# Fewer first-layer matmuls through take-outs, in a spectral-mixing and squared-ReLU kernel: 96 slots in fixed patterns, with new orders on three engines

## The chip, the cores and the metric

The kernel runs on one core of one Trainium2 chip. The metric is the device time of one execution in microseconds (us), lower is better. Each comparison runs the kernel before and the changed ones in turn on the same chip; different comparisons ran on different chips. The names of the engines in the profile are: PE for TensorE's matmuls and PEld for its weight loads, DVE for VectorE, ACT for ScalarE, POOL for GpSimd, SP for the engine that issues most DMAs. An "L" with a number is a line of the kernel.

## The reference

A real part of a two-dimensional Fourier transform over sequence and features, then a feed-forward layer with a squared ReLU.

```python
# x: (8, 3008, 256) f32; w_in: (256, 2048); w_out: (2048, 256)
X = np.fft.fft(np.fft.fft(x, axis=1), axis=2).real
x2 = X.reshape(8 * 3008, 256)
h = np.maximum(x2 @ w_in, 0.0)
out = (h * h) @ w_out           # (24064, 256) f32
```

## The kernel before

The feature transform is folded into the first weights (`G1`, `G2`, `G3`), the sequence transform makes two tables per batch, `pt` and `qt`. Column i of them serves two tokens, i and its mirror image: with A = G1 x pt and B = G2 x qt one token needs A+B, the other A-B. The 12040 columns are cut into 25 chunks. Chunks 2 to 23 have 512 columns and 8 slots each; a slot makes 256 of the 2048 hidden features for a chunk. The second layer's matmuls (`po`) of one chunk are spread over the slots of the next.

An ordinary slot uses three matmuls per 128 features: `G1` and `G2` give A+B, ScalarE reads it from PSUM, where the matmuls' results lie; `G3` (twice `G2`, negative, with other signs in one edge row) turns it into A-B, ScalarE reads again. A *take-out* slot saves the third one: after `G1`, VectorE takes A out of PSUM, doubled and with a correction for the edge row (`t`), TensorE adds `G2`, ScalarE reads A+B, and VectorE reads A+B again with `t` to make A-B. The correction is an *edge term* (`et`), made by POOL: a row of `qt`, spread to all 128 partitions by a DMA once per chunk (`eb`), times a number per feature.

```python
    def e_spread(c):                       # POOL issues the copy of the chunk's edge row
        ebc[c] = esp.tile([P, CH], F16, name="eb", tag="eb", bufs=2)
        for (b, i, o, l) in chunks[c][3]:
            nc.gpsimd.dma_start(out=ebc[c][:, o : o + l],
                in_=PQ[b][1][P - 1 : P, i : i + l].unsqueeze(1).to_broadcast([1, P, l]))
    def e_term(c, u):                      # two POOL multiplies of 128x512
        t = edge[c, u] = esp.tile([P, 2, CH], F16, name="et", tag="et", bufs=2)
        for j in range(2):
            f = 2 * u + j
            nc.gpsimd.tensor_scalar(out=t[:, j], in0=ebc[c], scalar1=gE2[:, f : f + 1],
                                    scalar2=None, op0=ALU.mult)
    # ... (x_front: G1, then VectorE takes out)
            stt(out=t, in0=xb, scalar=-2.0, in1=edge.pop((c, u)), op0=ALU.mult, op1=ALU.add)
    # ... (x_back, a take-out: TensorE has added G2)
        nc.vector._custom_dve(TENSOR_ADD_SAT, out=d[:, :, ::-1], in0=v, in1=t, s0=BIG, s1=0.0)
        act(r_s(c, u), v, AF.Relu, scale=-1.0)
    # ... (when they are issued; si is the step of slot u of chunk c)
    for si, (c, u) in enumerate(steps):
        if u == 0 and PLAN[c][0]:
            side.setdefault(si - (2 if len(chunks[c][3]) > 1 else 4), []).append(lambda c=c: e_spread(c))
    for si, (c, u) in enumerate(steps):
        if u in PLAN[c][0]:
            side.setdefault(si - 2, []).append(lambda c=c, u=u: e_term(c, u))
```

The schedule is manual: every engine runs its instructions in the order of this code. So a wait of POOL for one thing holds up everything behind it on POOL.

Of the kernel before, what the change touches and what calls it, by code (L numbers as in the profile page):

```python
# [10 lines left out]
F32 = mybir.dt.float32  # L11
F16 = mybir.dt.float16
I32 = mybir.dt.int32
AF = mybir.ActivationFunctionType
# [10 lines left out]
def kernel(  # L25
# [7 lines left out]
    nc = tc.nc  # L33
    B, S, D = x.shape
    _, F = moe_w_in.shape
    P = 128
# [10 lines left out]
    NFC = F // P  # L47
# [27 lines left out]
    def iota(name, shape, pattern, base, mult, dt=F32):  # L75
        t = const.tile(shape, dt, name=name)
        nc.gpsimd.iota(t, pattern=pattern, base=base, channel_multiplier=mult,
                       allow_small_or_imprecise_dtypes=True)
        return t
# [49 lines left out]
    for s in range(2):  # L129
        gather(0, 1 - s)  # L130
        nc.sync.dma_start(out=x4[0:NP, s, :, :], in_=up(0, s))
    jrow = iota("jrow", [P, P], [[1, P]], 1, 0)
    idx2 = iota("idx2", [P, 1], [[0, 1]], NQ // 2 * (NP - 1), -NQ // 2, I32)
    wout16 = const.tile([P, NFC, D], F16, name="wout16")
    wst = [h2p.tile([P, 2, F // 4], F32, name="wst", tag="h2") for _ in range(4)]
# [53 lines left out]

    def dmats():  # L190
        pv = nc.gpsimd
        t = tgp.tile([P, P], F32, name="td", tag="td")
        m = tgp.tile([P, P], F32, name="md", tag="md")
        pv.tensor_scalar(out=m, in0=jrow, scalar1=pidx[:, 0:1], scalar2=None, op0=ALU.mult)
        pv.tensor_scalar(out=t, in0=m, scalar1=1.0 / D, scalar2=R23, op0=ALU.mult, op1=ALU.add)
        pv.tensor_scalar(out=t, in0=t, scalar1=R23, scalar2=-float(D),
                         op0=ALU.subtract, op1=ALU.mult)
        pv.tensor_tensor(m, m, t, op=ALU.add)
        pv.memset(csD[:, 0, 0, P - 1 : P], 1.0)

        def fin():
            absval(t, m)
            nc.vector.tensor_copy(csD[:, 0, 1, P - 1 : P], alt)
            act(csD[:, 0, 1, 0 : P - 1], m[:, 0 : P - 1], AF.Sin, bias=0.0, scale=wD)
            act(csD[:, 0, 0, 0 : P - 1], t[:, 0 : P - 1], AF.Sin, bias=hpi[:, 0:1], scale=-wD)

        def hi():
            ts(out=csD[:, 1, :, 0:P:2], in0=csD[:, 0, :, 0:P:2], scalar1=-1.0, scalar2=None,
               op0=ALU.mult)
            nc.vector.tensor_copy(csD[:, 1, :, 1:P:2], csD[:, 0, :, 1:P:2])  # L210
        return fin, hi
# [270 lines left out]
        chunks.append((g, n, CH // n, segs, NFC // (2 * (CH // n))))  # L482
        g += n

    YZ = [(0, 0)] * 4 + [(3, 0)] * 2 + [(4, 1)] * 9 + [(5, 2)] * 9 + [(0, 0)]

    def plan(c, y, z):
        n = chunks[c][4]
        if chunks[c][1] != CH:
            return (), ()  # L490
        return ([u for u in range(n) if (u * y + 4) % n < y],
                [u for u in range(n) if (u * z + 6) % n < z])

    PLAN = [plan(c, *YZ[c]) for c in range(len(chunks))]

# [12 lines left out]
    def h2v(c, u):  # L508
        n, nf = chunks[c][1:3]
        if (c, u) not in h2t:  # L510
            t = h2p.tile([P, 4 * CH], F16, name="h2", tag="h2")
            h2t[c, u] = t[:, 0 : 4 * nf * n].rearrange("p (f t) -> p f t", f=2 * nf)
        return h2t[c, u]

    def mm2_ops(c):
        g0, n, nf, segs, _ = chunks[c]
        full = n // P * P
        tiles = [(s, t0, P) for s in range(2) for t0 in range(0, full, P)]
        groups = [tiles[i : i + 2] for i in range(0, len(tiles), 2)]
        if n > full:  # L520
            groups.insert(0, [(2, full, n - full)])
        ops = []
        st = {}

        def rows_out(s, t0, m, src):
            base = g0 + n - t0 - m if s else g0 + t0
            o = 0
            while o < m:
                b, i = divmod(base + o, NK)
                if i < NE:  # L530
                    l = min(m - o, NE - i)
                    kk = 2 * i
                else:
                    l = min(m - o, NK - i)
                    kk = 2 * (i - NE) + 1
                lo, hi = 0, l
                if s and kk == 0:
                    lo = 1
                if s and kk + 2 * (l - 1) == M:
                    hi = l - 1  # L540
                if hi > lo:
                    if s:
                        r0 = b * S + S - (kk + 2 * (hi - 1))
                        p0 = m - (o + hi)
                    else:
                        r0 = b * S + kk + 2 * lo
                        p0 = o + lo
                    nl = hi - lo
                    nc.sync.dma_start(out=out[r0 : r0 + 2 * nl - 1 : 2, :], in_=src(p0, nl))
                o += l  # L550

        def store(grp, po):
            os_ = osp.tile([P, 2, D], F32, name="os", tag="os")
            if grp[0][0] == 2:
                _, t0, m = grp[0]
                act(os_[0 : 2 * m, 0], po[0 : 2 * m, 0], AF.Copy, bias=0.0, scale=HS * HS)
                rows_out(0, t0, m, lambda p0, nl: os_[p0 : p0 + nl, 0, :])
                rows_out(1, t0, m, lambda p0, nl: os_[m + p0 : m + p0 + nl, 0, :])
                return
            act(os_, po, AF.Copy, bias=0.0, scale=HS * HS)  # L560
            for j, (s, t0, m) in enumerate(grp):
                rows_out(s, t0, m, lambda p0, nl, j=j: os_[p0 : p0 + nl, j, :])

        def one(grp, j, fc):
            s, t0, m = grp[j]

            def f():
                if j == 0 and fc == 0:
                    st["o"] = pso.tile([P, 2, D], F32, name="po", tag="po")
                o = n + n % P + t0 if s == 1 else t0  # L570
                w = 2 * m if s == 2 else m
                mm(st["o"][0:w, j, :], h2v(c, fc // (2 * nf))[:, fc % (2 * nf), o : o + w], wout16[:, fc, :],
                   fc == 0 and j == 0, fc == NFC - 1)
                if fc == NFC - 1 and j == len(grp) - 1:
                    return lambda o=st["o"]: store(grp, o)
            return f

        for grp in groups:
            ops += [one(grp, j, fc) for j in range(len(grp)) for fc in range(NFC)]
        return ops  # L580

    def relu_d(c, u, put):
# [9 lines left out]
    def r_s(c, u):  # L592
        return h2v(c, u)[:, :, 0 : chunks[c][1]]
# [24 lines left out]
    edge = {}  # L618

    def e_term(c, u):  # L620
        t = edge[c, u] = esp.tile([P, 2, CH], F16, name="et", tag="et", bufs=2)
        for j in range(2):
            f = 2 * u + j
            nc.gpsimd.tensor_scalar(out=t[:, j], in0=ebc[c], scalar1=gE2[:, f : f + 1], scalar2=None,  # L624
                                    op0=ALU.mult)
# [18 lines left out]
    def x_back(cur):  # L644
        c, u, xb, t = cur
        for j in range(2 * chunks[c][2]):
            x_mm(c, u, xb, j, G3 if t is None else G2, 1, False)
        v = x_view(c, xb)
        if t is None:
            relu_d(c, u, lambda o, i: act(o, v[:, :, i], AF.Relu, scale=-1.0))  # L650
            return
        d = h2v(c, u)[:, :, CH : 2 * CH]
        nc.vector._custom_dve(TENSOR_ADD_SAT, out=d[:, :, ::-1], in0=v, in1=t, s0=BIG, s1=0.0)  # L653
        act(r_s(c, u), v, AF.Relu, scale=-1.0)  # L654

    def x_square(cur):
        c, u = cur[:2]
# [108 lines left out]
    side.setdefault(10, []).append(e_double)  # L766
    for si, (c, u) in enumerate(steps):
        if u == 0 and PLAN[c][0]:
            side.setdefault(si - (2 if len(chunks[c][3]) > 1 else 4), []).append(lambda c=c: e_spread(c))
    for si, (c, u) in enumerate(steps):  # L770
        if u in PLAN[c][0]:
            side.setdefault(si - 2, []).append(lambda c=c, u=u: e_term(c, u))

    LAG = 1
    SQ = 1
# [7 lines left out]
    def retire():  # L783
        v = made.pop(0)
        x_square(v)
        if v[1] == chunks[v[0]][4] - 1:
            wait.append(v[0])

    for si, (c, u) in enumerate(steps):
        while wait:  # L790
            d = wait.pop(0)
            mmq += mm2_ops(d)
            due = si + chunks[d + 1][4]
        take = [mmq.pop(0) for _ in range(-(-len(mmq) // max(1, due - si)))]
        h = len(take) // 2
        posts = []
        if si in turn:
            posts += [f() for f in take[:h]]
        flight.append(x_front(c, u))
        if si not in turn:  # L800
            posts += [f() for f in take[:h]]
        if len(flight) > LAG:
            x_back(flight[0])
            made.append(flight.pop(0))
        posts += [f() for f in take[h:]]
        for p in posts:
            if p:
                p()
        while rest:
            rest.pop()()  # L810
        if len(made) > SQ:
            retire()
        for f in side.get(si, []):
            f()
    while flight:
# [42 lines left out]
```

## Time and profile before

| | before |
|---|---|
| median of the runs beside the changed kernel | 641.87 us (641.72 to 645.73, 4 runs) |
| span in the profile | 641.1 us |
| take-outs (edge terms) / ScalarE squares | 87 / 27 |

The page of the kernel before, part 1 (busy time of each engine, share of the span, instructions) and part 4 (the chain of waits that ended last, followed back from the end: share of the span by engine, then by engine and line):

```profile
PE 598.3 (93%) x4606; PEld 439.0 (68%) x4606; DVE 523.8 (82%) x650; ACT 417.9 (65%) x525; POOL 396.6 (62%) x269
...
PE 50%; DVE 12%; POOL 12%; DMA 7%; issue 5%; ACT 3%; DVEq 0%; SPq 0%; POOLq 0%; ACTq 0%
PE po L73 29%; PE xb L73 17%; POOL et L624 9%; DMA x<-in_x_dram 3%; DVE h L664 3%; DMA eb<-qt 3%; PE pf L73 3%; DVE h L653 2%; DVE t L639 2%; POOL x L101 2%; DVE u L328 2%; ACT h L650 1%; DVE v L340 1%; POOL x L124 1%; ACT os L560 1%
```

TensorE is the bound, but 12% of the chain lies on edge terms and the copies that feed them (9% + 3%).

The groups of instructions of the kernel before (count, then busy us, mean ns; then the idle time just before them and what ended it):

```profile
L73 PE MATMUL po<-wout,h 128*128 128x256 f16 x3024 | 394.1, 273 | 6.0 <-DVE h L664 6.0
L624 POOL TENSOR_SCALAR et<-eb,gE 128x512 f16<-128x512 f16 x174 | 327.9, 1897 | 106.3 <-DVE t L639 53.2
L653 DVE CUSTOM_DVE_ANT_0 h<-xb,t 128x1024 f16<-128x1024 f32 x87 | 106.2, 1221 | 29.4 <-PE xb L73 29.2
L639 DVE SCALAR_TENSOR_TENSOR t<-xb,et 128x1024 f32<-128x1024 f32 x87 | 105.9, 1219 | 18.8 <-POOL et L624 15.2
```

A take-out thus costs VectorE 1.22 + 1.22 us and POOL 2 x 1.90 us. The wait list of the kernel before (who waited for whom: us in total, times, longest):

```profile
ACT h L654 <- DVE h L653: 122.3, 77, 5.3
...
POOL et L624 <- DVE t L639: 53.2, 27, 3.8
POOL et L624 <- DMA eb<-qt: 46.5, 12, 7.8
...
DVE t L639 <- POOL et L624: 15.2, 12, 3.7
```

The timeline of POOL in the kernel before (start us, duration us, what, how many; in brackets the idle time before it and what ended it). The first copy here is for chunk 21, which straddles two batches and needs two; the others are for chunks 22 and 23:

```profile
525.37 3.10 POOL L624 TENSOR_SCALAR et<-eb,gE 128x512 f16<-128x512 f16 x2 [2.07 <-DVE t L639]
528.42 1.14 POOL L615 DMA_DIRECT2D eb<-qt  x2
535.72 14.13 POOL L624 TENSOR_SCALAR et<-eb,gE 128x512 f16<-128x512 f16 x8 [6.16 <-DMA eb<-qt]
549.80 0.59 POOL L615 DMA_DIRECT2D eb<-qt  x1
550.44 3.10 POOL L624 TENSOR_SCALAR et<-eb,gE 128x512 f16<-128x512 f16 x2
556.93 13.39 POOL L624 TENSOR_SCALAR et<-eb,gE 128x512 f16<-128x512 f16 x8 [3.40 <-DMA eb<-qt]
570.27 0.58 POOL L615 DMA_DIRECT2D eb<-qt  x1
571.77 3.10 POOL L624 TENSOR_SCALAR et<-eb,gE 128x512 f16<-128x512 f16 x2 [0.91 <-DVE t L639]
577.04 7.00 POOL L624 TENSOR_SCALAR et<-eb,gE 128x512 f16<-128x512 f16 x4 [2.18 <-DMA eb<-qt]
```

A copy's *flight*, from its issue to its landing, takes over 6 us (6.6 in the median, part 6 of the page). In chunk 21 nothing stands between issue and first term, and POOL idles 6.16 us. In chunks 22 and 23 one term of the chunk before (two multiplies, 3.1 us) stands between, and POOL idles 3.40 and 2.18 us.

### The profile page before, as it was taken

To read this page: it belongs to the slowest core of one execution; us is meant where nothing else is said; L and a number is where in the kernel's file an instruction comes from. 1 tells how busy PE (TensorE), PEld (TensorE's weight loads), DVE (VectorE), ACT (ScalarE), POOL (GpSimd) and SP (SyncE) were. 2 spreads that over 40 slices of the span, in tenths; PEclk is the share of its full clock that TensorE was granted. 3 is DMA by queue.
4 is the path that set the end of the run, shared out by engine and by line. 5 is a ranking of instruction groups with operands and counts; after the bars stand their busy time and mean duration, and the time that the engine had idled before them with its cause. 6 is when DMAs were issued, how large, how long until landed. Compare 5 with 4: busy or idle time off the path is not lost.

```text
span 641.1 us, 11481 instructions
## 1 busy us (share of the span) xinstructions
PE 598.3 (93%) x4606; PEld 439.0 (68%) x4606; DVE 523.8 (82%) x650; ACT 417.9 (65%) x525; POOL 396.6 (62%) x269
## 2 busy tenths in 40 slices
PE   3867998979999999899999999999999999999997
PEld 1545676656777777667777767866777767877786
DVE  8787696998898989789899879788787886888730
ACT  5865676455666676566765665766766676777771
POOL 8303043773778749978686758867587676789100
PEclk9989999899999999999999999999999999999999
DMA  8955367874196142941333131331431313431112
GB/s 264 295 93 135 110 159 198 147 186 83 51 179 116 50 58 38 221 69 51 46 55 41 52 40 52 59 42 34 58 48 45 58 50 42 58 57 52 50 51 67
DMA packets 37259, 57.05 MB, mean 89 GB/s; under 512 B 7214, under 2 KB 31442, under 8 KB 37206
## 3 DMA queue, kind: packets, MB, share of 16 engines
q0 software_dynamic: 7456, 30.08, 28.9%
q1 hardware_dynamic: 29702, 26.23, 13.0%
q8 instruction: 36, 0.59, 0.4%
q14 instruction: 17, 0.14, 0.1%
q10 hardware_dynamic: 48, 0.02, 0.0%
HBM read 29.02 MB, written 24.64 MB: 84 GB/s over the span
## 4 chain that ended last, share of the span: by engine, by line
PE 50%; DVE 12%; POOL 12%; DMA 7%; issue 5%; ACT 3%; DVEq 0%; SPq 0%; POOLq 0%; ACTq 0%
PE po L73 29%; PE xb L73 17%; POOL et L624 9%; DMA x<-in_x_dram 3%; DVE h L664 3%; DMA eb<-qt 3%; PE pf L73 3%; DVE h L653 2%; DVE t L639 2%; POOL x L101 2%; DVE u L328 2%; ACT h L650 1%; DVE v L340 1%; POOL x L124 1%; ACT os L560 1%
## 5 line engine op out<-in xcount | busy, mean ns | idle before, releaser
L73 PE MATMUL po<-wout,h 128*128 128x256 f16 x3024 | 394.1, 273 | 6.0 <-DVE h L664 6.0
L624 POOL TENSOR_SCALAR et<-eb,gE 128x512 f16<-128x512 f16 x174 | 327.9, 1897 | 106.3 <-DVE t L639 53.2
L73 PEld LDWEIGHTS <-h 128*128 128x128 f16 x3024 | 289.4, 98 | 98.2 <-DVE h L664 9.0
L664 DVE TENSOR_TENSOR h<-h 128x2048 f16<-128x2048 f16 (+1 forms) x165 | 201.2, 1220 | 16.2 <-ACT h L650 15.1
L73 PE MATMUL xb<-qt,G 128*128 128x512 f16 (+16 forms) x796 | 190.1, 321 | 9.3 <-DVE t L639 4.7
L654 ACT ACTIVATE h<-xb 128x1024 f16<-128x1024 f32 x87 | 89.2, 1025 | 123.9 <-DVE h L653 122.3
L73 PEld LDWEIGHTS <-G 128*128 128x128 f16 x1308 | 119.3, 98 | 69.8 <-issue 19.9
L73 PE MATMUL xb<-pt,G 128*128 128x512 f16 (+16 forms) x512 | 131.2, 323 | 10.0 <-ACT h L654 3.2
L653 DVE CUSTOM_DVE_ANT_0 h<-xb,t 128x1024 f16<-128x1024 f32 x87 | 106.2, 1221 | 29.4 <-PE xb L73 29.2
L641 ACT ACTIVATE h<-xb 128x1024 f16<-128x1024 f32 (+1 forms) x105 | 104.4, 994 | 33.4 <-PE xb L73 33.1
L650 ACT ACTIVATE h<-xb 128x1024 f16<-128x1024 f32 (+1 forms) x113 | 104.9, 937 | 29.5 <-PE xb L73 29.0
L639 DVE SCALAR_TENSOR_TENSOR t<-xb,et 128x1024 f32<-128x1024 f32 x87 | 105.9, 1219 | 18.8 <-POOL et L624 15.2
L560 ACT ACTIVATE os<-po 128x512 f32<-128x512 f32 x94 | 56.0, 596 | 9.4 <-PE po L73 6.3
L124 POOL DMA_DIRECT2D x<-in_x_dram x14 | 8.2, 586 | 78.8 <-DVE u L332 77.8
L328 DVE TENSOR_TENSOR u<-x 127x765 f16<-127x765 f32 x32 | 30.4, 975 | 5.5 <-DMA x<-in_x_dram 4.8
L101 POOL DMA_INDIRECT x<-in_x_dram,idx x18 | 27.8, 1545 | 5.5 <-issue 4.5
L662 ACT ACTIVATE h<-h 128x1024 f16<-128x1024 f16 x27 | 28.6, 1061 | 0.0
L661 ACT ACTIVATE h<-h 128x1024 f16<-128x1024 f16 x27 | 28.5, 1055 | 0.0
L73 PEld LDWEIGHTS <-w 127*128 127x128 f16 (+1 forms) x192 | 22.5, 120 | 8.6 <-DVE w L346 1.6
L346 DVE TENSOR_TENSOR w<-v 127x381 f16<-127x381 f16 x64 | 22.6, 385 | 0.0
L396 ACT ACTIVATE as<-pf 128x377 f32<-128x377 f32 (+5 forms) x32 | 15.6, 487 | 8.0 <-PE pf L73 6.6
L73 PE MATMUL pf<-cosT,w 127*128 127x377 f16 (+1 forms) x96 | 19.2, 336 | 0.8 <-DVE w L346 0.8
(101 smaller groups left out, 199.1 us busy)
## 6 DMA issues: line engine op xcount, KB each, us to landing
out_dram<-os SPq DMA_DIRECT2D x157, 128.0 KB
x<-in_x_dram POOLq DMA_DIRECT2D x14, 756.0 KB, 10.6
wst<-in_moe_w_in_dram POOLq DMA_DIRECT2D x4, 512.0 KB, 7.2
wot<-in_moe_w_out_dram POOLq DMA_DIRECT2D x4, 512.0 KB
eb<-qt POOLq DMA_DIRECT2D x14, 128.0 KB, 6.6
x<-in_x_dram SPq DMA_DIRECT2D x2, 756.0 KB
x<-in_x_dram,idx POOLq DMA_INDIRECT x18, 12.0
gE<-G SPq DMA_DIRECT2D x16, 0.2 KB
```

The source lines that it names most:

```text
L73: nc.tensor.matmul(o, l, r, start=start, stop=stop, skip_group_check=True)
L101: nc.gpsimd.indirect_dma_start(out=x4[0:NP, 2 + s, q : q + rows, :].rearrange("p q d -> p (q d)"), out_offset=None, in_=bass.AP(tensor=x.t ...
L328: return lambda: vt(u[k, s, q0 : q0 + NQ // 2, 1:D], x4[k, s, q0 : q0 + NQ // 2, 1:D], x4[k, 3 - s, ::-1, :][:, q0 : q0 + NQ // 2, D - 1 : ...
L560: act(os_, po, AF.Copy, bias=0.0, scale=HS * HS)
L624: nc.gpsimd.tensor_scalar(out=t[:, j], in0=ebc[c], scalar1=gE2[:, f : f + 1], scalar2=None, op0=ALU.mult)
L639: stt(out=t, in0=xb, scalar=-2.0, in1=edge.pop((c, u)), op0=ALU.mult, op1=ALU.add)
L641: act(r_s(c, u), x_view(c, xb), AF.Relu, scale=-1.0)
L650: relu_d(c, u, lambda o, i: act(o, v[:, :, i], AF.Relu, scale=-1.0))
L653: nc.vector._custom_dve(TENSOR_ADD_SAT, out=d[:, :, ::-1], in0=v, in1=t, s0=BIG, s1=0.0)
L654: act(r_s(c, u), v, AF.Relu, scale=-1.0)
L662: rest.append(lambda: act(h2[:, nf:], h2[:, nf:], AF.Square))
L664: vt(h2, h2, h2, op=ALU.mult)
```

## The change

Its intent: nine more take-outs, to spare TensorE matmuls; to pay for them on VectorE and POOL with better orders: ScalarE reads the sums first, squares move ahead of the VectorE sum, terms are made three steps ahead into three buffers, the second layer uses the last tile late.

```diff
-    YZ = [(0, 0)] * 4 + [(3, 0)] * 2 + [(4, 1)] * 9 + [(5, 2)] * 9 + [(0, 0)]
+    TAKE = {0: (), 3: (1, 4, 6), 4: (1, 3, 4, 6), 5: (1, 2, 4, 5, 6), 6: (0, 1, 2, 4, 5, 6)}
+    SQA = {0: (), 1: (4,), 2: (1, 5), 3: (1, 4, 6)}
+    YZ = [(0, 0)] * 4 + [(3, 0)] * 2 + [(5, 1)] * 18 + [(0, 0)]
 ...   (before, slots by formula: y=3: 2 4 7; y=4: 1 3 5 7; y=5: 0 1 3 4 6)
         for grp in groups:
-            ops += [one(grp, j, fc) for j in range(len(grp)) for fc in range(NFC)]
+            for fcs in (range(NFC - 2 * nf), range(NFC - 2 * nf, NFC)):
+                ops += [one(grp, j, fc) for j in range(len(grp)) for fc in fcs]
 ...
-        t = edge[c, u] = esp.tile([P, 2, CH], F16, name="et", tag="et", bufs=2)
+        t = edge[c, u] = esp.tile([P, 2, CH], F16, name="et", tag="et", bufs=3)
 ...
+        act(r_s(c, u), v, AF.Relu, scale=-1.0)
         nc.vector._custom_dve(TENSOR_ADD_SAT, out=d[:, :, ::-1], in0=v, in1=t, s0=BIG, s1=0.0)
-        act(r_s(c, u), v, AF.Relu, scale=-1.0)
 ...
-            side.setdefault(si - (2 if len(chunks[c][3]) > 1 else 4), []).append(lambda c=c: e_spread(c))
+            one = len(chunks[c][3]) == 1
+            late = chunks[c][3][-1][0] - 1 in EGRP
+            side.setdefault(si - (4 if one else 2 if late else 3), []).append(lambda c=c: e_spread(c))
 ...
-            side.setdefault(si - 2, []).append(lambda c=c, u=u: e_term(c, u))
+            side.setdefault(si - 2 - (u > 0), []).append(lambda c=c, u=u: e_term(c, u))
 ...
         if si in turn:
-            posts += [f() for f in take[:h]]
+            posts += [f() for f in take]
+            take = []
         flight.append(x_front(c, u))
-        if si not in turn:
-            posts += [f() for f in take[:h]]
+        posts += [f() for f in take[:h]]
+        if len(made) > SQ - 1:
+            retire()                 # the square, ahead of the VectorE sum (before: after it)
         if len(flight) > LAG:
             x_back(flight[0])
```

Cut: two small scratch tiles of the start move into a buffer that is free then, which makes room for the third `et` buffer.

More of the change, by code (lines that the diff above doesn't have):

```diff
@@ L131 @@
         nc.sync.dma_start(out=x4[0:NP, s, :, :], in_=up(0, s))
-    jrow = iota("jrow", [P, P], [[1, P]], 1, 0)
+    jm = h2p.tile([P, 3, P], F32, name="jm", tag="h2")
+    jrow = jm[:, 0]
+    nc.gpsimd.iota(jrow, pattern=[[1, P]], base=1, channel_multiplier=0,
+                   allow_small_or_imprecise_dtypes=True)
     idx2 = iota("idx2", [P, 1], [[0, 1]], NQ // 2 * (NP - 1), -NQ // 2, I32)
@@ L191, in dmats @@
         pv = nc.gpsimd
-        t = tgp.tile([P, P], F32, name="td", tag="td")
-        m = tgp.tile([P, P], F32, name="md", tag="md")
+        t, m = jm[:, 1], jm[:, 2]
         pv.tensor_scalar(out=m, in0=jrow, scalar1=pidx[:, 0:1], scalar2=None, op0=ALU.mult)
@@ L483 @@
         g += n
-    YZ = [(0, 0)] * 4 + [(3, 0)] * 2 + [(4, 1)] * 9 + [(5, 2)] * 9 + [(0, 0)]
+    TAKE = {0: (), 3: (1, 4, 6), 4: (1, 3, 4, 6), 5: (1, 2, 4, 5, 6), 6: (0, 1, 2, 4, 5, 6)}
+    SQA = {0: (), 1: (4,), 2: (1, 5), 3: (1, 4, 6)}
+    YZ = [(0, 0)] * 4 + [(3, 0)] * 2 + [(5, 1)] * 18 + [(0, 0)]
     def plan(c, y, z):
-        n = chunks[c][4]
-        if chunks[c][1] != CH:
-            return (), ()
-        return ([u for u in range(n) if (u * y + 4) % n < y],
-                [u for u in range(n) if (u * z + 6) % n < z])
+        return TAKE[y], SQA[z]
     PLAN = [plan(c, *YZ[c]) for c in range(len(chunks))]
@@ L810 @@
             rest.pop()()
-        if len(made) > SQ:
-            retire()
         for f in side.get(si, []):
```

## The prediction

> **What bounds the kernel now.** TensorE: the page has it busy 598 of 641 us. Its matmuls start about 109 ns (256 columns) and 216 ns (512) apart; so spaced, all need about 581 us, so it starves for about 45 us: 27 us before 160 us, some 17 us after. VectorE is busy 524 us, ScalarE 418, GpSimd (POOL) 397. The chain of waits already runs 9% through the edge terms (`et`, POOL) and 3% through the copies that spread an edge row (`eb`). The wait list has POOL waiting 46 us for `eb` (12 waits), VectorE 15 for `et`.
>
> **What the change does.** One more take-out in each of chunks 6 to 14. Each spares two 512-column matmuls (TensorE -4 us in all) and adds two VectorE passes of 1.22 us (22 us) and two POOL multiplies of 1.90 us (34 us). ScalarE squares drop from 27 to 18: ScalarE -19 us, VectorE +11. Reading PSUM on ScalarE first ends the 122 us that ScalarE waits behind VectorE, but ScalarE has slack. Using the last tile late removes TensorE's 6 us wait for squares. Three `et` buffers loosen POOL's 53 us wait for VectorE. All this alone gains 5 to 12 us.
>
> **What it costs.** In the new instruction order each chunk's `eb` copy is issued after the previous chunk's last edge term and directly before its own first one; before, in one-batch chunks, a term or more lay between. POOL runs in order, so it idles for the whole flight: the timeline has 5.8 to 7.8 us from the end of the issue to the next term where nothing lies between. POOL's cycle per chunk becomes five terms, an issue and a full wait:
> - chunks 15 to 23: 5 x 3.5 + 0.8 + 6.3 = about 24.7 us, against 24.1 us per chunk measured now;
> - chunks 6 to 14: terms are slower, about 4.0 us (the Trainium skill, "GPSIMD Engine Reference", section 1, says that POOL shares SBUF interfaces with VectorE and contends with instructions of two SBUF inputs; this trace agrees: a multiply takes 1.55 us at best, 2.0 to 2.2 us here, 1.7 to 1.8 us later). So 20 + 0.8 + 6.3 = 27 us, plus some 12 us in all for two batches' input loads, against 24.9 us now.
>
> Laid end to end from chunk 6 (158 us), POOL is done near 635 us, not 597, and 40 us of work follow. My estimate: POOL bounds from chunk 6 on; gains elsewhere vanish.
>
> **Prediction.** 674 us, range 650 to 692. Chances: faster by over 2% 0.05, within 2% 0.13, slower by over 2% 0.82.
>
> **What would show it.** POOL's waits for `eb` rise from 46 to about 100 us in about 18 waits; its wait for VectorE's `t` falls to near nothing; VectorE's wait for `et` grows from 15 to over 60 us; the chain of waits runs mostly through `et` and `eb`; chunks 6 to 14 lengthen by over 2 us each, 15 to 23 by under 1.5; TensorE's busy share falls below 92%. Separately: ScalarE's 122 us wait near zero; TensorE's wait for squares gone after 100 us.
>
> **What would make it wrong.** Faster multiplies (1.7 us throughout would bring the time to about 645 us); a shorter flight of `eb`; or a lead from three buffers that hides more. Then VectorE, 24.5 of 24.9 us per chunk in 6 to 14, is the next limit, and the time stays within 2%.

## The result

The changed kernel takes 679.14 us (677.19 to 682.51, 4 runs) against 641.87; the ratio is 1.0571, 95% interval 1.0513 to 1.0629. A ratio here is the mean time of one kernel's runs over that of the other's of the same rounds, so not quite the ratio of the medians quoted.

The page of the changed kernel, parts 1, 4 and two groups of part 5:

```profile
PE 602.7 (89%) x4582; PEld 437.6 (65%) x4582; DVE 554.4 (82%) x677; ACT 394.4 (58%) x498; POOL 439.7 (65%) x287
...
POOL 41%; DMA 17%; PE 14%; DVE 12%; issue 4%; ACT 2%; POOLq 0%; DVEq 0%; ACTq 0%
POOL et L625 39%; DMA eb<-qt 13%; PE po L73 8%; PE xb L73 5%; DVE h L665 4%; DMA x<-in_x_dram 4%; DVE h L655 3%; DVE t L640 2%; PE pf L73 2%; POOL x L101 1%; DMA qt<-es 1%; DVE u L330 1%; ACT h L654 1%; DVE v L342 1%; DVE w L348 1%
...
L625 POOL TENSOR_SCALAR et<-eb,gE 128x512 f16<-128x512 f16 x192 | 374.6, 1966 | 111.3 <-DMA eb<-qt 104.7
L73 PE MATMUL po<-wout,h 128*128 128x256 f16 x3024 | 387.1, 273 | 0.0
```

The chain has gone over from TensorE (50% to 14%) to POOL's terms and the copies' flights (12% to 52% together). POOL's own busy share is still only 65%. That is a mean over stages: from 158 to 638 us POOL is busy 372 of 480 us (77%) and waits another 94 us for `eb`, and waiting is not busy time.

The wait list of the changed kernel:

```profile
POOL et L625 <- DMA eb<-qt: 104.7, 17, 11.1
...
DVE t L640 <- POOL et L625: 42.0, 31, 5.2
ACT h L662 <- DVE h L655: 38.1, 18, 3.2
PE xb L73 <- DVE h L655: 27.9, 29, 6.1
...
DVE h L655 <- ACT h L654: 17.0, 31, 1.6
...
PE xb L73 <- DVE t L640: 12.5, 19, 1.9
```

POOL waits for nearly every chunk's copy (17 times, mean 6.2 us) and no longer for VectorE's `t`. VectorE then waits for POOL, and TensorE for VectorE. The timeline of POOL in the changed kernel, from the copy for chunk 19 to the terms of chunk 21:

```profile
509.65 0.59 POOL L616 DMA_DIRECT2D eb<-qt  x1
516.52 17.19 POOL L625 TENSOR_SCALAR et<-eb,gE 128x512 f16<-128x512 f16 x10 [6.28 <-DMA eb<-qt]
533.66 0.59 POOL L616 DMA_DIRECT2D eb<-qt  x1
540.73 18.91 POOL L625 TENSOR_SCALAR et<-eb,gE 128x512 f16<-128x512 f16 x10 [6.48 <-DVE h L655]
559.58 1.14 POOL L616 DMA_DIRECT2D eb<-qt  x2
567.42 18.89 POOL L625 TENSOR_SCALAR et<-eb,gE 128x512 f16<-128x512 f16 x10 [6.70 <-DMA eb<-qt]
```

This is a closed cycle: ten multiplies, an issue, a flight, ten multiplies. (The bracket at 540.73 names VectorE. The term waits for a free buffer and for the copy, and the gap is as long as those put down to the copy.) In this stretch POOL is never without either work or a flight to wait for.

The time by stretch, worked out from the traces: chunk limits are the starts of each chunk's first `xb<-pt` matmul, counted in program order. TensorE's starvation is the sum, over neighbouring matmul starts, of their distance less columns/2.4 ns and 2.2 ns (that is what they take back to back in these traces, 109 ns for 256 columns, 216 ns for 512); time lost to a lower granted clock counts in it too. Chunk 24 ends here with the last matmul, 3.8 us before the span's end.

| us | start to chunk 5 | chunks 6-14 | chunks 15-23 | chunk 24 | TensorE starved in 6-14 / 15-23 |
|---|---|---|---|---|---|
| before | 164.0 | 224.0 | 216.8 | 32.4 | 7.4 / 9.8 |
| changed | 164.3 | 249.5 | 227.3 | 32.6 | 36.7 / 20.2 |

### The profile page after: what moved, and what is told of

It reads as the page before. It is cut to its first block, busy times and chain, and to the rows that moved or that the text cites. A ratio compares the mean times of both kernels' runs of the same rounds, so it can differ in the third digit from the quotient of the medians.

```text
span 677.4 us, 11458 instructions
## 1 busy us (share of the span) xinstructions
PE 602.7 (89%) x4582; PEld 437.6 (65%) x4582; DVE 554.4 (82%) x677; ACT 394.4 (58%) x498; POOL 439.7 (65%) x287
## 4 chain that ended last, share of the span: by engine, by line
POOL 41%; DMA 17%; PE 14%; DVE 12%; issue 4%; ACT 2%; POOLq 0%; DVEq 0%; ACTq 0%
POOL et L625 39%; DMA eb<-qt 13%; PE po L73 8%; PE xb L73 5%; DVE h L665 4%; DMA x<-in_x_dram 4%; DVE h L655 3%; DVE t L640 2%; PE pf L73 2%; POOL x L101 1%; DMA qt<-es 1%; DVE u L330 1%; ACT h L654 1%; DVE v L342 1%; DVE w L348 1%
## 5 line engine op out<-in xcount | busy, mean ns | idle before, releaser
L625 POOL TENSOR_SCALAR et<-eb,gE 128x512 f16<-128x512 f16 x192 | 374.6, 1966 | 111.3 <-DMA eb<-qt 104.7
L73 PE MATMUL po<-wout,h 128*128 128x256 f16 x3024 | 387.1, 273 | 0.0
L665 DVE TENSOR_TENSOR h<-h 128x2048 f16<-128x2048 f16 (+1 forms) x174 | 210.6, 1212 | 15.4 <-ACT h L651 14.1
L73 PE MATMUL xb<-qt,G 128*128 128x512 f16 (+16 forms) x772 | 184.2, 322 | 16.8 <-DVE t L640 12.5
L73 PE MATMUL xb<-pt,G 128*128 128x512 f16 (+16 forms) x512 | 130.5, 324 | 40.5 <-DVE h L655 27.9
L640 DVE SCALAR_TENSOR_TENSOR t<-xb,et 128x1024 f32<-128x1024 f32 x96 | 117.0, 1218 | 45.5 <-POOL et L625 42.0
L651 ACT ACTIVATE h<-xb 128x1024 f16<-128x1024 f32 (+1 forms) x104 | 96.1, 932 | 72.3 <-PE xb L73 72.1
L642 ACT ACTIVATE h<-xb 128x1024 f16<-128x1024 f32 (+1 forms) x96 | 95.3, 993 | 65.7 <-PE xb L73 65.5
L654 ACT ACTIVATE h<-xb 128x1024 f16<-128x1024 f32 x96 | 98.1, 1021 | 60.7 <-PE xb L73 59.0
L655 DVE CUSTOM_DVE_ANT_0 h<-xb,t 128x1024 f16<-128x1024 f32 x96 | 117.1, 1219 | 17.6 <-ACT h L654 17.0
L662 ACT ACTIVATE h<-h 128x1024 f16<-128x1024 f16 x18 | 19.0, 1057 | 38.1 <-DVE h L655 38.1
L616 POOL DMA_DIRECT2D eb<-qt x26 | 15.2, 585 | 11.3 <-DMA qt<-es 11.3
## 6 DMA issues: line engine op xcount, KB each, us to landing
x<-in_x_dram,idx POOLq DMA_INDIRECT x18, 12.7
```

The source lines that it names most:

```text
L73: nc.tensor.matmul(o, l, r, start=start, stop=stop, skip_group_check=True)
L642: act(r_s(c, u), x_view(c, xb), AF.Relu, scale=-1.0)
L651: relu_d(c, u, lambda o, i: act(o, v[:, :, i], AF.Relu, scale=-1.0))
L665: vt(h2, h2, h2, op=ALU.mult)
```

## The experiments

Theory A: POOL's chain, five terms per chunk plus the whole flight of the copy, is the bound. Rival B: the extra VectorE work (take-outs and squares) is. Rival C: the new order costs, which TensorE's 27.9 us wait for the VectorE sum suggests. All edits are of the changed kernel if not said otherwise, and all results were correct.

### e1_early_spread: the copies two terms earlier

```diff
-            side.setdefault(si - (4 if one else 2 if late else 3), []).append(lambda c=c: e_spread(c))
+            side.setdefault(si - (2 if late else 6), []).append(lambda c=c: e_spread(c))
```

> The changed kernel with one edit: each eb copy is issued six steps ahead of its chunk, so that two edge terms (four multiplies, about 7.5 us) lie between the copy and the first term that needs it; only the two chunks whose row is made late keep their place. The work on every engine is the same. Theory A (POOL's chain of five terms plus the whole flight of the copy is the bound): POOL's waits for eb fall from 105 us to under 25 us, and the time falls from 679 to 632-648 us. Rival B (nine more take-outs and nine more squares overload VectorE): VectorE's work is unchanged, so the time stays at 672-683 us. Rival C (ScalarE ahead of VectorE on PSUM holds VectorE up, which the trace shows as TensorE waiting 28 us for the VectorE sum): the order is unchanged, so 672-683 us.

Measured: 657.69 us, ratio to before 1.0248 (1.0230 to 1.0267). It recovers 21 us with no work changed on any engine, so B and C alone are out; but it missed the range of A, and POOL still waited 34.0 us for `eb`, not under 25. One cause was in the edit: the `late` rule also caught the whole chunks 7, 8, 16 and 17, whose copies now came two steps ahead and flew exposed as before (chunk 7 took 34.8 us, chunk 16 28.6). The mended run is e5.

### e2_vector_first: VectorE reads the sums first again

```diff
-        act(r_s(c, u), v, AF.Relu, scale=-1.0)
         nc.vector._custom_dve(TENSOR_ADD_SAT, out=d[:, :, ::-1], in0=v, in1=t, s0=BIG, s1=0.0)
+        act(r_s(c, u), v, AF.Relu, scale=-1.0)
```

> The changed kernel with VectorE reading the sums in PSUM ahead of ScalarE again, as in the kernel before; all else as changed. Theory A: POOL's chain is untouched, so the time stays within 6 us of 679, and ScalarE's wait behind VectorE comes back (about 120 us). Rival C (the new order is what costs): the time falls by 15 us or more, to 664 us or less. Rival B: no change.

Measured: 691.85 us, ratio to before 1.0786 (1.0760 to 1.0812). All three expectations missed: undoing the order makes the changed kernel 12.7 us slower. So C is not merely absent; ScalarE-first is a gain in this setting. The wait list of e2 shows how:

```profile
ACT h L655 <- DVE h L654: 218.9, 86, 5.5
...
DVE h L665 <- ACT h L655: 47.3, 49, 1.1
PE xb L73 <- ACT h L655: 42.2, 49, 2.3
```

The two readers of a sum run one after the other whichever is first: in neither trace do the two reads of any of the 96 sums overlap. With VectorE first, and the square next on VectorE, the squares and TensorE wait for ScalarE's late read.

### e3_takeouts_87: four take-outs in chunks 6 to 14

```diff
-    YZ = [(0, 0)] * 4 + [(3, 0)] * 2 + [(5, 1)] * 18 + [(0, 0)]
+    YZ = [(0, 0)] * 4 + [(3, 0)] * 2 + [(4, 1)] * 9 + [(5, 1)] * 9 + [(0, 0)]
```

> The changed kernel with four take-outs instead of five in chunks 6 to 14 (87 in all, as before), same squares, same place of the eb copies. Theory A: POOL's cycle loses one term of about 4 us in each of these nine chunks, so they come down from 27.7 us to about 24.5-25.5 us each, and chunks 15 to 23 stay at about 25.2 us each: 650-660 us in all, still slower than the kernel before by over 1%. Rival B: VectorE's load per chunk falls back to that of before in chunks 6 to 14, and in 15 to 23 it stays one square above: the time falls to 645 us or less.

Measured: 652.45 us, ratio 1.0158 (1.0137 to 1.0179), in A's range and above B's 645. Chunks 6 to 14 fall to 223.6 us, as in the kernel before; chunks 15 to 23, which keep five terms, stay at 224.7.

### e4_before_late_spread: the kernel before, with exposed copies

```diff
-            side.setdefault(si - (2 if len(chunks[c][3]) > 1 else 4), []).append(lambda c=c: e_spread(c))
+            side.setdefault(si - 2 + PLAN[c][0][0], []).append(lambda c=c: e_spread(c))
```

> The kernel before with one edit: each eb copy is issued directly ahead of the first edge term that needs it, so that nothing lies between. All else as before. Theory A: POOL's waits for eb rise from 46 to 90 us or more, and the time rises to 648-660 us without any of the other parts of the change. Rivals B and C: VectorE's load and the order on PSUM are those of before, so the time stays at 640-645 us.

Measured: 684.80 us, ratio 1.0662 (1.0641 to 1.0684). More than any theory said, and so a warning. The timeline of POOL in e4 at chunk 5:

```profile
146.24 0.56 POOL L124 DMA_DIRECT2D x<-in_x_dram  x1 [1.50 <-DVE u L332]
147.10 1.03 POOL L101 DMA_INDIRECT x<-in_x_dram,idx  x1 [0.30 <-issue]
148.14 1.05 POOL L120 DMA_DIRECT2D x<-in_x_dram  x2
149.18 0.58 POOL L615 DMA_DIRECT2D eb<-qt  x1
161.84 10.22 POOL L624 TENSOR_SCALAR et<-eb,gE 128x512 f16<-128x512 f16 x6 [12.08 <-DMA eb<-qt]
```

The edit had put this copy behind a batch's input loads, and its flight was 12.1 us instead of some 6.3. The same happened at chunks 4, 7 and 10 (waits of 11.6, 9.1 and 7.4 us, on copies that the loads had already put off), and the loss sits there: 17.5 us up to chunk 5, and in chunks 6 to 14 all of the 20.7 us is in chunks 7 and 10, which took 37.4 and 38.5 us instead of 26.1 and 29.1. So this run does not measure the plain exposure; e11 does.

Nor need the loss be the flights' alone. The granted clock in 40 slices of the span (part 2 of the pages, tenths of full speed), first of the kernel before, then of e4:

```profile
PEclk9989999899999999999999999999999999999999
...
PEclk9999999599998899988999999999999999999999
```

In chunks 4, 5, 7 and 10 of e4 the mean granted clock was 0.81, 0.95, 0.86 and 0.87, in the kernel before 0.95 in chunk 4 and 1.00 in the others. Each dip came while or after TensorE stood idle for 5.5 to 11 us on end. That share of the clock is worth at most some 20 us of these chunks' time (an estimate: clock missing times length); the runs do not separate it from the flights.

### e5_early_all: e1, mended

```diff
-            side.setdefault(si - (4 if one else 2 if late else 3), []).append(lambda c=c: e_spread(c))
+            side.setdefault(si - (2 if late and not one else 6), []).append(lambda c=c: e_spread(c))
```

> As the run with early copies, mended: there four whole chunks (7, 8, 16, 17) had been caught by the rule for late rows and were issued two steps ahead, with the whole flight exposed again; now only chunks 6 and 15 are. Theory A (POOL's chain with the exposed flight accounts for the change's loss): POOL's waits for eb fall from 34 to under 15 us, chunks 7 and 16 come down from 34.8 and 28.6 us to about 27 and 26, and the time is 638-648 us. If VectorE's nine extra take-outs are a second limit (theory A with a remainder), chunks 6 to 14 stay over 25.5 us each on average, against 24.9 in the kernel before, and the time stays at 645 or above. Rival B in full (VectorE alone explains the loss): 655 us or above.

Measured: 647.48 us, ratio to before 1.0088 (1.0056 to 1.0119). Placing the copies two terms earlier brings back 31.7 of the 37.3 us. The time is in A's range; POOL's waits for `eb` (17.2 us, not under 15) and chunk 7 (28.5 us, not about 27) are a little over what was expected. The chain (part 4 of its page) and waits of e5:

```profile
PE 48%; DVE 30%; issue 6%; ACT 4%; DMA 2%; POOL 0%; DVEq 0%; ACTq 0%
PE po L73 27%; PE xb L73 18%; DVE h L665 11%; DVE h L655 7%; DVE t L640 6%; PE pf L73 3%; DVE u L330 3%; DMA x<-in_x_dram 2%; ACT h L654 2%; ACT h L662 1%; DVE w L348 1%; DVE v L342 1%; ACT h L651 0%; DVE pt L434 0%; DVE eall L358 0%
```

```profile
POOL et L625 <- DVE t L640: 43.0, 18, 4.2
...
POOL et L625 <- DMA eb<-qt: 17.2, 3, 12.2
...
PE xb L73 <- DVE h L655: 12.9, 25, 1.3
```

POOL is off the chain, although its multiplies have grown slower (2.03 us on average, 1.97 in the changed kernel). It waits for VectorE again, not the other way round. Half of TensorE's wait for the VectorE sum went with it, though the order is the same: that wait was passed on from POOL. But a remainder appeared: chunks 6 to 14 take 234.8 us, 26.1 each, with VectorE busy 219.6 us of it (94%).

### e6_early_87: early copies and four take-outs in chunks 6 to 14

```diff
-    YZ = [(0, 0)] * 4 + [(3, 0)] * 2 + [(5, 1)] * 18 + [(0, 0)]
+    YZ = [(0, 0)] * 4 + [(3, 0)] * 2 + [(4, 1)] * 9 + [(5, 1)] * 9 + [(0, 0)]
-            side.setdefault(si - (4 if one else 2 if late else 3), []).append(lambda c=c: e_spread(c))
+            side.setdefault(si - (2 if late and not one else 6), []).append(lambda c=c: e_spread(c))
```

> The same with four take-outs in chunks 6 to 14 (87 in all). Theory A with a remainder on VectorE: this is faster than the 96 take-outs with early copies by 5-15 us, TensorE is the bound nearly everywhere after 160 us, and the time is 628-636 us, better than the kernel before (642). Theory A without a remainder: within 4 us of the run with 96 take-outs and early copies.

Measured: 638.37 us, ratio to before 0.9932 (0.9904 to 0.9960). It is 9.1 us faster than e5, so the nine take-outs do cost time even with hidden flights: chunks 6 to 14 take 223.9 us with VectorE busy 200.2 (89%). They load VectorE and POOL alike; that VectorE is the limit is read from e5's chain (DVE 30%, POOL 0%) and not tested alone. The time misses the range by 2 us.

### e7_before_early: the kernel before, with nothing but early copies

```diff
-            side.setdefault(si - (2 if len(chunks[c][3]) > 1 else 4), []).append(lambda c=c: e_spread(c))
+            one = len(chunks[c][3]) == 1
+            late = chunks[c][3][-1][0] - 1 in EGRP
+            side.setdefault(si - (2 if late and not one else 6), []).append(lambda c=c: e_spread(c))
```

> The kernel before with nothing but the early copies (all chunks but 6 and 15). Theory A: in the kernel before the flights cost little, since a term or more lay in front of most of them: TensorE's starvation in the chunks that straddle two batches (1.2 to 2.2 us each in 9, 15, 18, 21) goes, and the time is 632-639 us. If it falls under 632, the flights cost the kernel before more than its chain showed.

Measured: 632.43 us, ratio to before 0.9854 (0.9826 to 0.9882), the fastest median of all. The kernel before had itself lost 9.6 us to exposed flights (1.2 us between the two profiles lie in chunk 1 and are rather the clock's, see e12). Part 4 of its page:

```profile
PE 61%; DVE 12%; POOL 7%; issue 5%; ACT 3%; DMA 2%; DVEq 0%; ACTq 0%; POOLq 0%
PE po L73 36%; PE xb L73 22%; POOL et L624 4%; PE pf L73 3%; DVE h L664 3%; DVE t L639 3%; DVE h L653 2%; DMA x<-in_x_dram 2%; DVE u L328 2%; POOL x L101 2%; ACT h L650 1%; DVE v L340 1%; POOL x L124 1%; POOL x L120 1%; ACT h L654 0%
```

The flights have left the chain. It also sets a second question: e6, which has the same number of take-outs and the same early copies plus the rest of the change, is 6 us slower.

### e8_early_87_tile_in_turn: e6 without the late last tile

```diff
-            for fcs in (range(NFC - 2 * nf), range(NFC - 2 * nf, NFC)):
-                ops += [one(grp, j, fc) for j in range(len(grp)) for fc in fcs]
+            ops += [one(grp, j, fc) for j in range(len(grp)) for fc in range(NFC)]
```

> The run with 87 take-outs and early copies, with the second layer taking a chunk's tiles in turn again, as before. If the late last tile is worth what TensorE's waits for squares showed (6.0 us in the kernel before, 0 in the changed one), this is 2-6 us slower than the run with the late tile; TensorE's wait for VectorE's squares ahead of the second layer comes back.

Measured: 637.87 us, ratio to before 0.9926 (0.9898 to 0.9953), the same as e6. Missed: the late tile is worth nothing here. With the squares made earlier, the wait that it removes had already shrunk: the group `po` waits 1.9 us for squares in e8, 6.0 in the kernel before, 0.0 in e6.

### e9_early_87_even: e6 with the slots of before

```diff
-    TAKE = {0: (), 3: (1, 4, 6), 4: (1, 3, 4, 6), ...
+    TAKE = {0: (), 3: (2, 4, 7), 4: (1, 3, 5, 7), ...
```

> As the run with 87 take-outs and early copies (638.4 us), with the take-outs of chunks 4 to 14 spread as in the kernel before (slots 1, 3, 5, 7 instead of 1, 3, 4, 6; in chunks 4 and 5 slots 2, 4, 7). That run is 6 us slower than the kernel before with early copies (632.4 us), 4 of them in chunks 6 to 14, about 1 us in each chunk that straddles two batches. If the neighbouring slots 3 and 4 do it (VectorE gets two take-outs in a row), chunks 6 to 14 come back to about 219.6 us and the time is 629-634 us. If the new order on VectorE and ScalarE does it, the time stays at 635-640 us.

Measured: 638.67 us, ratio to before 0.9947 (0.9929 to 0.9966). Neighbouring slots are not the cause; chunks 6 to 14 take 225.6 us.

### e10_before_early_order: e7 with only the new orders

On top of e7, of the change the fourth hunk (ScalarE first) and the last (squares ahead; second-layer matmuls ahead in steps with a transform):

```diff
+        act(r_s(c, u), v, AF.Relu, scale=-1.0)
         nc.vector._custom_dve(TENSOR_ADD_SAT, out=d[:, :, ::-1], in0=v, in1=t, s0=BIG, s1=0.0)
-        act(r_s(c, u), v, AF.Relu, scale=-1.0)
 ...
+        if len(made) > SQ - 1:
+            retire()
         if len(flight) > LAG:
             x_back(flight[0])
 ...
-        if len(made) > SQ:
-            retire()
```

> The kernel before with early copies (632.4 us) and, of the rest of the change, only the new orders: ScalarE reads the sums first, squares ahead of the VectorE sum, and all second-layer matmuls ahead of the first layer in steps with a transform. Take-outs, squares, tile order and buffers are those of before. If the order helps only where VectorE is overloaded (undoing ScalarE-first cost the changed kernel 12.7 us), it is worth nothing here: 630-635 us. If it is a gain of its own: 629 us or less. If it costs by itself: 635 us or more.

Measured: 637.16 us, ratio to before 0.9909 (0.9888 to 0.9930): slower than e7 by 4.7 us in the medians. The orders cost where folding for later batches also loads VectorE (chunks 6 to 14: 223.6 us, in e7 219.6) and gain where it doesn't (15 to 23: 210.9, in e7 213.1); that the folding is the reason was not tested. The profiles differ by another 5.1 us before chunk 6, 3.5 of them in chunk 1 and rather the clock's (see e12); without chunk 1 the two profiles are 3.4 us apart. Which of the three orders does it was not separated.

### e11_before_exposed: e4, mended

The kernel before, each copy directly after the last term of the chunk before and ahead of the input loads; in the list of side work the loop over terms comes first, then:

```diff
+            last = max(PLAN[c - 1][0], default=6)
+            if late and not one:
+                side.setdefault(si - 2, []).insert(0, lambda c=c: e_spread(c))
+            else:
+                side.setdefault(si - 10 + last, []).append(lambda c=c: e_spread(c))
```

> The earlier run that put the eb copies of the kernel before directly ahead of their first term (684.8 us) also put three of them behind a batch's input loads, and those flights took 9 to 12 us. Here each copy stands after the last term of the chunk before, as in the changed kernel, and ahead of the input loads. Theory A with its own arithmetic: four terms of 4.2 us, an issue and a flight are about 24 us in chunks 6 to 14, less than the 24.9 us per chunk that TensorE and VectorE take there, and about 24.5 us with five terms in chunks 15 to 23; so a whole flight is nearly affordable with four terms: 640-652 us, POOL's waits for eb over 80 us. If the flight alone costs what the 684.8 us seemed to say: 665 us or more.

Measured: 645.80 us, ratio to before 1.0054 (1.0036 to 1.0071), as A's arithmetic said. POOL waits for copies nearly as long as in the changed kernel (104.7), at a tenth of the loss:

```profile
POOL et L624 <- DMA eb<-qt: 91.3, 15, 8.0
```

With four terms the cycle nearly fits.

### e12_early_new_order_late: the best of both

Early copies as in e5; the orders, slots and squares of the kernel before up to chunk 14, those of the changed kernel from chunk 15 on:

```diff
+        if c >= 15:
+            act(r_s(c, u), v, AF.Relu, scale=-1.0)
         nc.vector._custom_dve(TENSOR_ADD_SAT, out=d[:, :, ::-1], in0=v, in1=t, s0=BIG, s1=0.0)
-        act(r_s(c, u), v, AF.Relu, scale=-1.0)
+        if c < 15:
+            act(r_s(c, u), v, AF.Relu, scale=-1.0)
 ...   (the same switch for retire() and the second layer's place; slots and squares by YZ)
```

> A kernel that should beat both: early copies; the orders, slots and squares of the kernel before up to chunk 14, the changed kernel's from chunk 15 on, three et buffers and 87 take-outs. Up to chunk 14 it should run as the kernel before with early copies, and chunks 15 to 23 in 210.9 instead of 213.1 us: 629-633 us.

Measured: 632.85 us, ratio to before 0.9851 (0.9828 to 0.9874). The time is in the range. It beats the kernel before by 1.5% and the changed one by 6.8% in the medians, but not e7: in its profile chunks 15 to 23 are 2.2 us shorter than in e7's, as expected, and chunk 1, which has no take-outs, is 2.7 us longer. Chunk 1 took 19.1 to 22.6 us over all 14 profiles, in step with the granted clock: 19.1 us in the five where the clock stayed whole in it, 20.3 to 20.8 in the four with 3.4 us at half clock, 21.4 to 21.8 in the four with 6.8 us (e12 is one), 22.6 in the one with 10.2 us (e10). e5 and e6 show the same TensorE pauses in chunk 1 and yet 0 and 6.8 us at half clock, so it is not the kernel's doing as far as these traces tell. Up to 3.5 us between two profiles can thus be the clock in chunk 1; for the medians the share is not known.

## Why the prediction was right

The time (674 said, 679 measured) and its mechanism held. Point by point:

- **POOL becomes the bound through the exposed flights.** Shown twice: the chain's POOL and copy share rose from 12% to 52%, and e5, which only moves the copies, gives back 31.7 us of 37.3.
- **POOL's cycle.** Said: a term of 4.0 us in chunks 6 to 14 and 3.5 later, POOL done near 635 us. Measured: 4.01 us (90 multiplies in 180.6 us), 3.73 us (90 in 167.9), done at 638.0 us. The later terms were underestimated by 0.2 us each, 10 us over 45 of them. That the end came out within 3 us is partly luck: POOL reached the copy for chunk 15 at 404.7 us, 8 us ahead of the 413 that the prediction's sum gives, and took 233 us from there, not 222.
- **By stretch.** Said: over 2 us more per chunk in 6 to 14, under 1.5 in 15 to 23. Measured: 2.8 and 1.2.
- **Named waits.** POOL for `eb` about 100 us in 18: 104.7 in 17. POOL for `t`: gone from 53.2. TensorE's busy share 89%, under 92%. ScalarE's 122 us behind VectorE's sum and TensorE's wait for squares: gone, though ScalarE's 18 squares now wait 38.1 us for VectorE. VectorE for `et`: 42.0, not over 60, missed; what TensorE lost is listed under its waits for VectorE's sum (27.9) and `t` (12.5), which VectorE passes on.
- **VectorE as the next limit, within 2%.** e5: +0.9%, VectorE 94% busy in chunks 6 to 14.

**What failed is the step "All this alone gains 5 to 12 us".** With the flights hidden the change still loses: e5 is 5.5 us slower than the kernel before and 15.1 slower than e7, the kernel before with the same early copies. I had weighed TensorE's sparing and the removed waits, and put VectorE down as a limit only as a way to be wrong. Terms of that sum, as measured: nine take-outs cost 9.1 us with early copies (e5 against e6) though they spare TensorE 4; the late tile is worth nothing (e8); the new orders cost about 4.7 us in the kernel before with early copies (e10 against e7), while one of them, ScalarE first, saves 12.7 in the changed kernel (e2). "ScalarE has slack" was true and beside the point: what the order decides is what VectorE and TensorE wait for.

The two causes do not add up independently. In the changed kernel's family, medians in us (the kernel before had medians of 641.9 to 642.5 whenever it ran beside one of these, so medians are compared across sets of runs):

| | copies as changed | copies early | flights cost |
|---|---|---|---|
| 87 take-outs | 652.45 (e3) | 638.37 (e6) | 14.1 |
| 96 take-outs | 679.14 | 647.48 (e5) | 31.7 |
| nine take-outs cost | 26.7 | 9.1 | |

With four terms in chunks 6 to 14 the exposed flight is free there (223.6 us in e3, 223.9 in e6); with five it costs 14.7 (249.5 against 234.8), or 1.6 us a chunk. With the orders of before even four terms leave a small price (224.7 us in e11, 219.6 in e7; 3.6 of these 5.1 us are in chunk 10, where e11 also had 3.4 us at half clock). A cycle of four terms and a flight, 4 x 4.0 + 0.8 + 6.3 = 23 us, is shorter than the 24.9 us that the other engines take; one of five is longer. Neither part shows its price alone: e11 has almost all of the flights and is 0.5% slower than the kernel before (13.4 us slower than e7, most of it in chunks 15 to 23, which have five terms).

The books: the changed kernel's flights +31.7, less the 9.6 that the kernel before lost to its own (e7), nine take-outs +9.1, the rest of the change +6.0 (e6 against e7): 37.2 of 37.3 us. They add up by construction, each run standing once on either side; they split the loss and do not prove it. Of the rest, the tile order (e8) and the slots (e9) are out and the orders make up some 4.7 us (e10). The squares moved from ScalarE to VectorE and the third `et` buffer with its earlier terms were not tested singly.

## What to carry to other kernels

On an in-order engine, add up the whole cycle, work and flights that it waits through, and compare it with what the others take per turn: an engine with a busy share of 65% can be the bound. A wait costs little while the cycle is shorter than the others' turn, and above that only the excess: a flight of 6.3 us cost 1.6 us a chunk in chunks 6 to 14 here. Where a transfer is issued decides what its flight hides behind, so read the instruction order and not only the step numbers; two terms of work in between were worth more here than every other part of the change. A wait that an engine passes on carries the wrong name: test the first engine of the chain.

## What the Trainium skill lacked or had wrong

- "DMA: Bandwidth & Descriptors", section on the anatomy of one DMA on the SWDGE path, gives about 2.0 us plus bytes over 436 GB/s, which would be some 2.3 us for these 128 KB (an estimate from that page). The page doesn't say which transfers it was fitted on. The spreading of one SBUF row to 128 partitions, issued from GpSimd, took 6.6 us (kernel before) and 6.9 us (changed) from issue to landing, in the median; the page has no number for this case.
- That page has no number for what a small copy pays behind large loads on the same issuing engine: a wait of 12.1 us in e4 against some 6.3 alone.
- "GPSIMD Engine Reference", section 1, names the contention with VectorE's instructions of two SBUF inputs; that section gives no size (another page of the skill says more on the sharing). Here a 128x512 fp16 multiply by a scalar per partition took 1.55 us at best, 1.90 us on average before and 2.03 in e5, and up to 3.3 us. The trace of the kernel before agrees with the contention: 33 multiplies that none of VectorE's two-input instructions on SBUF (`h`, `w`, `u`) overlapped took 1.56 us on average and 1.58 at most, the 30 that such ones overlapped for over 1.3 us took 2.37.
- "Trainium Kernel Development and Optimization", best practices, says of engines other than TensorE, where the distance to the roofline is judged, that "occupancy is fine". Nothing here contradicts that as a measure of the distance to the roofline, but it doesn't find the bound: from 158 to 638 us POOL bounded the changed kernel at 77% busy (65% of the whole span), while TensorE was 91% busy (439 of 480 us), since waits for DMA flights do not count as busy.
